# Attention values in four column groups of the PE array, with the first 64-key product carrying values and sums together

## The chip, the cores and the metric

One core of a Trainium2 chip runs the kernel. The time is device microseconds of one execution, the median of several runs. Engines are named as the profile names them: PE (matmul; PEld is its weight load), DVE (vector), ACT (scalar), POOL, SP, and the DMA queues that SP and POOL issue to.

## The reference, cut to what matters

Attention over 4 batches, 12 heads, 448 positions and 64 channels, all float32, with a soft cap on the scores, followed by a two-layer network with squared ReLU:

```
scores = cap * tanh(scale * q @ k.T / cap)
p      = exp(scores - max)
attn   = p / (sum(p) + 1e-9)
y      = attn @ v                       # (4, 12, 448, 64)
x      = heads of y side by side        # (1792, 768)
out    = (max(x @ w_in, 0) ** 2) @ w_out  # 768 -> 2048 -> 768
```

## The kernel before, in words

The program has three stages. The attention stage treats 24 pairs of heads (two heads of one batch fill the 128 partitions, 64 channels each). The second and third stages are the two matrix products of the network, in a Strassen form; a planner writes out their order from costs and due times, and starts with leftovers of attention (the last normalisations). The first units of the second stage run on PE straight behind the last pair.

The attention loop (L597) is software-pipelined by hand, and each engine executes its instructions in the order written. In cycle n:

- PE computes the scores of pair n transposed (keys on partitions), in three pieces of 128 keys (`scores`, L397) and, in even cycles, the remaining 64 keys of this pair and the next one in one piece (`half_scores`, L404). Then it multiplies the probabilities of pair n-1 with the values: `pv_half` (L437) opens the two accumulators `pa` (values of both heads) and `pb` (sums of the probabilities, by a matrix of ones) with the 64-key piece; `sums` (L448) adds to `pb`, by four 32-column matmuls, what DVE has added up of the other three pieces; `pv` (L455) adds those pieces to `pa`, with two 64-column matmuls for each.
- ACT applies tanh to each score piece and exp to two tiles a cycle; in cycles 5 to 16 it casts a finished x as well (L509), and now and then it decodes a piece of `w_in`.
- DVE adds the probability tiles (`add_p`, `add_p3`), transposes the next queries and keys (`turn_kq`, L390), copies `pb` out (`take_sums`, L467) and `pa` out (`evac`, L462), inverts the sums (`invert`, L474) and multiplies (`normalise`, L493).
- The sums travel: two DMAs on SP take them from one row for each half of the queries to a compact tile of 32 x 28 (`cmp`), which DVE inverts, a third puts it to DRAM (`rd`), and two on POOL (`spread`, L482) copy it to 64 partitions each, beside the values in `e`, where `normalise` finds it one cycle later.

`pa` and `pb` are one PSUM bank each and single-buffered; the `es` tile that `take_sums` writes is single-buffered too. `e` has three buffers. The kernel alternates the halves of partitions that the two heads' last 64 keys occupy from pair to pair (`rows`, `v_slot`, L364 to L376).

Of the kernel before, what the change touches and what calls it, by code (L numbers as in the profile page):

```python
# [240 lines left out]
def tile_softcap_attention_mlp(ctx, tc, q, k, v, cap, w_in, w_out, out):  # L241
# [42 lines left out]
    ep = rctx.enter_context(tc.tile_pool(name="ep", bufs=2))  # L284
    scr = rctx.enter_context(tc.tile_pool(name="scr", bufs=1))
# [13 lines left out]
    guard = const.tile([P, 1], F32, name="guard")  # L299
# [10 lines left out]
    vn = [keep.tile([P, NS + 1, D], F32, name=f"vn{i}") for i in range(NKV)]  # L310
# [4 lines left out]
    def prepare():  # L315

        nc.vector.memset(ones, 1.0)

# [4 lines left out]

    def fetch_w(pool, f, first, bufs):
        raw = new_raw(pool, bufs)
        if first:
            nc.sync.dma_start(
                out=raw.rearrange("p (c f) -> p c f", f=P),
                in_=w_in[:, f * P:(f + 1) * P].rearrange("(c p) f -> p c f", p=P),
            )  # L330
        else:
            nc.sync.dma_start(out=raw, in_=w_out[f * P:(f + 1) * P])
        return raw
# [18 lines left out]
    top, bottom = slice(0, D), slice(D, P)  # L352

    def load_part(n, i, a, queue):
        b, j = divmod(n, NPAIR)
        h, w = divmod(a, 2)
        x = (k, q)[i][b, 2 * j + h, :, 32 * w:32 * w + 32].rearrange("(t r) e -> r t e", r=32)
        queue.dma_start(out=kqn[n % NKQ][32 * a:32 * a + 32, i], in_=x)  # L358
# [5 lines left out]
    def rows(n, h):  # L364
        return bottom if (n + h) % 2 else top

    def keys(n, h, u):
        odd = (n + h) % 2
        if u:
            return slice(odd * D + (u - 1) * P, odd * D + u * P)  # L370
        return slice(0, D) if odd else slice(3 * P, S)

    def v_slot(n, h, u):
        if n % 2 == 0:
            return (0, 4)[h] + u - 1 if u else 3
        return (1, 4)[h] + u - 1 if u else (0, 7)[h]  # L376

    def load_v(n):
        b, j = divmod(n, NPAIR)
        x = v[b, 2 * j:2 * j + 2].rearrange("h (t r) d -> (h t) r d", r=D)  # L380
        for i in range(2):
            r, at = (bottom, 0) if (n + i) % 2 else (top, n % 2)
            nc.gpsimd.dma_start(out=vn[n % NKV][r, at:at + NS], in_=x[i::2].rearrange("t r d -> r t d"))  # L383
# [13 lines left out]
    def scores(n, u):  # L397
        sc = ps_s.tile([P, 2, 512], F32, tag="s", name="sc")
        kt, qt = kqs[n][:, :S], kqs[n][:, S:]
        for h, r in enumerate((top, bottom)):  # L400
            nc.tensor.matmul(out=sc[:, h, :S], lhsT=kt[r, keys(n, h, u)], rhs=qt[r], start=True, stop=True)  # L401
        probs[n, u] = sc

    def half_scores(n):  # L404
        sc = ps_s.tile([P, 2, 512], F32, tag="s", name="sc")
        for i in range(2):
            kt, qt = kqs[n + i][:, :S], kqs[n + i][:, S:]
            for h, r in enumerate((top, bottom)):
                nc.tensor.matmul(out=sc[rows(n + i, h), i, :S], lhsT=kt[r, keys(n + i, h, 0)], rhs=qt[r],  # L409
                                 start=True, stop=True)  # L410
# [26 lines left out]
    def pv_half(n):  # L437
        pvs[n, 0] = ps_v.tile([P, S], F32, tag="pa", name="pa")
        pvs[n, 1] = ps_v.tile([P, S], F32, tag="pb", name="pb")
        p = probs.pop((n, 0))  # L440
        for h, o in enumerate((top, bottom)):
            r = rows(n, h)
            nc.tensor.matmul(out=pvs[n, 0][o], lhsT=vn[n % NKV][r, v_slot(n, h, 0)], rhs=p[r], start=True, stop=False)  # L443
        for h, o in enumerate((bottom, top)):
            r = rows(n, h)
            nc.tensor.matmul(out=pvs[n, 1][o], lhsT=ones[r], rhs=p[r], start=True, stop=False)

    def sums(n):  # L448
        a = adds.pop(n)
        for i in range(4):  # L450
            h, c = 1 - i // 2, slice(i % 2 * HS, (i % 2 + 1) * HS)
            nc.tensor.matmul(out=pvs[n, 1][32 * i:32 * i + 32, c], lhsT=ones[:, :32], rhs=a[:, h, c],  # L452
                             start=False, stop=True, tile_position=(0, 32 * i))

    def pv(n):  # L455
        for u in range(1, NU):
            p = probs.pop((n, u))
            for h, r in enumerate((top, bottom)):
# [850 lines left out]
```

## Time and profile before

| | us |
|---|---|
| median of 3 runs (586.91 to 587.23) | 586.96 |
| the profiled execution, its time | 587.03 |
| the profiled execution, its span | 585.4 |
| PE busy in the span | 576.9 |
| DVE busy | 463.8 |
| ACT busy | 380.2 |
| POOL busy | 156.1 |

Busy time of PE is modelled and says little by itself; the attention stage lies between about 8 and 175 us of the span, and what follows is the network. How busy an engine is has to be read by stage: the rows below give it in pieces of the attention loop.

### The profile page before, as it was taken

The numbers are of one execution on the slowest core, as the hardware profiler recorded it, in microseconds if no ns is written. First come the engines' busy times: TensorE is split into PE (matmuls) and PEld (weight loads), VectorE is DVE, ScalarE is ACT, GpSimd is POOL, SyncE is SP. The second block draws the span as 40 slices with busy tenths as digits, with TensorE's granted clock in tenths as the row PEclk, the third lists the DMA queues.
The fourth block names the chain that finished last, engine by engine and source line by source line (L and its number), as shares of the span: only waits on it lengthen the run. The fifth ranks groups of instructions, "written<-read, shape, count | busy, mean of one in ns | idle before, by whom it ended". The sixth has DMA issues, their size and how long they took to land.

```text
span 585.4 us, 9055 instructions
## 1 busy us (share of the span) xinstructions
PE 576.9 (99%) x3286; PEld 458.2 (78%) x3286; DVE 463.8 (79%) x607; ACT 380.2 (65%) x437; POOL 156.1 (27%) x245
## 2 busy tenths in 40 slices
PE   8999999999999999999999999999999999999996
PEld 5333333333349999999999999999999999999996
DVE  2778889899969989979789983756899996766651
ACT  4999999999958877577667763765635543333230
POOL 8688787886421001120211211100000000000000
PEclk9999999999999999999999999999999999999999
DMA  9989999899215235886879778997899236544511
GB/s 133 134 160 167 172 179 156 171 156 171 83 51 161 111 117 203 261 269 225 265 243 330 241 264 302 318 335 255 247 279 289 71 109 209 148 142 146 169 40 45
DMA packets 138997, 110.18 MB, mean 188 GB/s; under 512 B 53728, under 2 KB 127968, under 8 KB 138944
## 3 DMA queue, kind: packets, MB, share of 16 engines
q1 hardware_dynamic: 125408, 71.86, 46.9%
q0 software_dynamic: 12000, 37.39, 23.3%
q8 instruction: 27, 0.44, 0.3%
q10 hardware_dynamic: 1536, 0.27, 0.3%
q14 instruction: 26, 0.21, 0.1%
HBM read 82.84 MB, written 26.56 MB: 187 GB/s over the span
## 4 chain that ended last, share of the span: by engine, by line
PE 93%; DMA 2%; DVE 2%; ACT 1%; issue 0%; SPq 0%; POOL 0%; ACTq 0%; DVEq 0%; POOLq 0%
PE hps L349 35%; PE po L1141 35%; PE pa L459 9%; PE sc L401 8%; PE pa L443 3%; PE pb L452 2%; PE sc L409 1%; DMA cap_sb<-in_cap_dram 1%; DMA cmp<-es 1%; ACT p L427 1%; ACT p L419 1%; DMA wraw<-in_moe_w_in_dram 1%; DVE es L469 0%; SPq L472 0%; POOL kqn L358 0%
## 5 line engine op out<-in xcount | busy, mean ns | idle before, releaser
L1141 PE MATMUL po<-th,gh 128*128 128x384 f32 x728 | 190.2, 336 | 0.0
L1141 PEld LDWEIGHTS po<-th,gh 128*128 128x128 f32 x728 | 131.9, 188 | 0.0
L1141 PE MATMUL po<-th,gl 128*128 128x384 f32 x392 | 131.7, 336 | 0.0
L1130 ACT CAST gh<-a 128x1024 fp32r<-128x1024 f32 x47 | 49.4, 1052 | 97.3 <-PE po L1141 90.4
L349 PE MATMUL hps<-xt,op 128*128 128x448 f32 x450 | 92.4, 362 | 0.0
L349 PEld LDWEIGHTS hps<-xt,op 128*128 128x128 f32 x450 | 84.4, 187 | 5.6
L419 ACT ACTIVATE p<-sc 128x896 f32<-128x896 f32 x84 | 73.4, 908 | 10.2 <-PE sc L401 10.0
L1141 PEld LDWEIGHTS po<-th,gl 128*128 128x128 f32 x392 | 73.7, 188 | 0.0
L427 ACT ACTIVATE p<-p 128x1792 f32<-128x1792 f32 (+1 forms) x48 | 72.5, 1511 | 1.3
L1131 DVE TENSOR_TENSOR gl<-a,gh 128x1024 fp32r<-128x1024 f32 x47 | 57.4, 1222 | 19.0 <-ACT gh L1130 19.0
L349 PE MATMUL hps<-xs,op 128*128 128x448 f32 x324 | 67.6, 363 | 0.0
L349 PEld LDWEIGHTS hps<-xs,op 128*128 128x128 f32 x324 | 60.6, 188 | 5.4 <-issue 1.4
L401 PE MATMUL sc<-kq 64*128 64x448 f32 x288 | 61.0, 555 | 0.9 <-DVE kq L394 0.7
L358 POOL DMA_DIRECT2D kqn<-in_k_dram x92 | 59.0, 648 | 2.5 <-issue 1.5
L459 PE MATMUL pa<-p,vn 128*64 128x448 f32 x288 | 59.4, 548 | 0.0
L401 PEld LDWEIGHTS sc<-kq 64*128 64x128 f32 x288 | 25.6, 186 | 35.4 <-issue 18.6
L349 PE MATMUL hps<-xh,op 128*128 128x448 f32 x168 | 49.4, 362 | 0.0
L383 POOL DMA_DIRECT2D vn<-in_v_dram x48 | 35.2, 739 | 31.8 <-PE pa L459 31.4
L459 PEld LDWEIGHTS pa<-p,vn 128*64 128x64 f32 x288 | 18.5, 136 | 30.9 <-issue 30.9
L1154 DVE TENSOR_TENSOR osb<-s,po 128x384 f32<-128x384 f32 x27 | 14.9, 552 | 27.4 <-PE po L1141 27.3
L48 DVE CUSTOM_DVE_ANT_0 wf<-wraw,wf 128x1536 uint16<-128x1536 uint16 x32 | 30.4, 949 | 3.7 <-ACT wraw L43 1.7
L40 ACT ACTIVATE wf<-wraw 128x768 f32<-128x768 f32 x32 | 29.1, 911 | 6.3 <-DVE op L831 4.3
(94 smaller groups left out, 838.5 us busy)
## 6 DMA issues: line engine op xcount, KB each, us to landing
a<-g_dram SPq DMA_DIRECT2D x56, 512.0 KB
wraw<-in_moe_w_out_dram SPq DMA_DIRECT2D x16, 768.0 KB
wraw<-in_moe_w_in_dram SPq DMA_DIRECT2D x12, 768.0 KB
g_dram<-r POOLq DMA_DIRECT2D x18, 448.0 KB, 5.0
g_dram<-u POOLq DMA_DIRECT2D x14, 448.0 KB, 5.1
w_dram<-wf POOLq DMA_DIRECT2D x16, 384.0 KB, 5.9
vn<-in_v_dram POOLq DMA_DIRECT2D x48, 112.0 KB, 4.3
e<-rd POOLq DMA_DIRECT2D x48, 112.0 KB, 3.7
```

Of the source, the lines that this page charges most:

```text
L40: size=lambda: nc.scalar.activation(out=magf, in_=high.bitcast(F32), func=ACTF.Abs, scale=2.0 ** 16),
L48: total=lambda: V.tensor_tensor(out=mag, in0=mag, in1=low, op=ALU.add),
L349: nc.tensor.matmul(out=out, lhsT=w, rhs=x[:, j], start=start and c == 0 and s == 0, stop=stop and c == NHALF - 1 and s == 2, skip_group_ch ...
L358: queue.dma_start(out=kqn[n % NKQ][32 * a:32 * a + 32, i], in_=x)
L383: nc.gpsimd.dma_start(out=vn[n % NKV][r, at:at + NS], in_=x[i::2].rearrange("t r d -> r t d"))
L401: nc.tensor.matmul(out=sc[:, h, :S], lhsT=kt[r, keys(n, h, u)], rhs=qt[r], start=True, stop=True)
L419: nc.scalar.activation(out=p, in_=probs[n, u][:, :, :S], func=ACTF.Tanh, scale=by["qks"])
L427: nc.scalar.activation(out=p, in_=p, func=ACTF.Exp, scale=by["cap"])
L459: nc.tensor.matmul(out=pvs[n, 0][r], lhsT=vn[n % NKV][:, v_slot(n, h, u)], rhs=p[:, h], start=False, stop=(u == NU - 1))
L1130: last["act"] = nc.scalar.copy(out=hi, in_=x)
L1131: last["dve"] = nc.vector.tensor_sub(out=lo, in0=x, in1=f32(hi))
L1141: last["mm"] = nc.tensor.matmul(out=po, lhsT=w[:, c], rhs=m[:, cols], start=(c == 0 and i == 0), stop=(c == HF - 1 and i == 2))
```

## The change

The probabilities' sums and values now share one accumulator of two banks, `pv`, one bank for each head. Head 1's values lie on partitions 0 to 63 of bank 1 and head 0's on partitions 64 to 127 of bank 0; the other half of each bank takes the sums. The value tile gets a column block of ones at both ends, so that `pv_half` is two matmuls of 64 rows by 128 columns (values and sums together) in place of four of 64 by 64. `pv` uses four matmuls of 32 columns for each piece of 128 keys in place of two of 64, and runs ahead of `sums`. One DVE instruction over both banks, `evac`, adds the guard (1e-9, on the rows of sums only) and copies; `take_sums` and its tile are gone. Two DMAs collect two full rows of 448 each, so that `cmp` has 64 rows; it is inverted at the end of the next cycle, and `spread` is issued at the end of a cycle, in POOL's order still behind the same loads. Heads no longer alternate by pair where the values are concerned, but in the places of queries and keys (`head`); the rows of `w_in` are fetched with their halves of 64 exchanged, by two transfers for each column block. The planner's ready times for the last two pairs change with it.

```diff
+    def head(n, place):
+        return place if n % 2 else 1 - place
...
     def pv_half(n):
-        pvs[n, 0] = ps_v.tile([P, S], F32, tag="pa", name="pa")
-        pvs[n, 1] = ps_v.tile([P, S], F32, tag="pb", name="pb")
+        pvs[n] = ps_v.tile([P, 2, 512], F32, tag="pv", name="pv")
         p = probs.pop((n, 0))
-        for h, o in enumerate((top, bottom)):
-            r = rows(n, h)
-            nc.tensor.matmul(out=pvs[n, 0][o], lhsT=vn[n % NKV][r, v_slot(n, h, 0)], rhs=p[r], start=True, stop=False)
-        for h, o in enumerate((bottom, top)):
-            r = rows(n, h)
-            nc.tensor.matmul(out=pvs[n, 1][o], lhsT=ones[r], rhs=p[r], start=True, stop=False)
+        for h, slot in enumerate((0, NS + 1)):
+            w = vn[n % NKV][rows[h], slot:slot + 2].rearrange("p t d -> p (t d)")
+            nc.tensor.matmul(out=pvs[n][:, h, :S], lhsT=w, rhs=p[rows[h]], start=True, stop=False)
...
     def pv(n):
         for u in range(1, NU):
             p = probs.pop((n, u))
-            for h, r in enumerate((top, bottom)):
-                nc.tensor.matmul(out=pvs[n, 0][r], lhsT=vn[n % NKV][:, v_slot(n, h, u)], rhs=p[:, h],
-                                 start=False, stop=(u == NU - 1))
+            for i in range(4):
+                h, c = 1 - i // 2, quarter(i % 2)
+                nc.tensor.matmul(out=pvs[n][quarter(i), h, :S], lhsT=vn[n % NKV][:, 1 + 3 * h + u, c], rhs=p[:, h],
+                                 start=False, stop=(u == NU - 1), tile_position=(0, 32 * i))
...
     def evac(n):
-        es[n] = ep.tile([P, 2, S], F32, tag="u", name="e", bufs=3)
-        nc.vector.tensor_copy(out=es[n][:, 0], in_=pvs.pop((n, 0)))
-
-    def take_sums(n):
-        e = ep.tile([P, S], F32, tag="es", name="es", bufs=1)
-        nc.vector.tensor_scalar(out=e, in0=pvs.pop((n, 1)), scalar1=guard, scalar2=None, op0=ALU.add)
+        e = es[n] = ep.tile([P, 2, S], F32, tag="u", name="e", bufs=3)
+        nc.vector.tensor_tensor(out=e, in0=pvs.pop(n)[:, :, :S], in1=guard.unsqueeze(2).to_broadcast([P, 2, S]), op=ALU.add)
         rds[n] = ep.tile([NC, HB], F32, tag="cmp", name="cmp", bufs=NE)
-        for c in range(2):
-            nc.sync.dma_start(out=rds[n][c * (NC // 2):(c + 1) * (NC // 2)], in_=e[32 * c:P:64, c * HS:(c + 1) * HS])
+        for h in range(2):
+            nc.sync.dma_start(out=rds[n][h * NC // 2:(h + 1) * NC // 2], in_=e[D * h:D * h + D:32, h])
...
     for n in range(NP + 1):
...
-        if n >= 3:
-            spread(n - 3)
...
-        if n >= 2:
-            invert(n - 2)
...
         if old:
+            pv(n - 1)
             sums(n - 1)
-            take_sums(n - 1)
+        if old:
             fetch_early(n)
-            pv(n - 1)
...
         split_low(n - 5)
+        if n >= 3:
+            spread(n - 3)
         if old:
             evac(n - 1)
+        if n >= 2:
+            invert(n - 2)
...
-    spread_a = do("POOL", 0.7, lambda: spread(NP - 2), ready=4.0, lag=6.5)
-    invert_b = do("DVE", 0.6, lambda: invert(NP - 1), ready=6.5, lag=2.5)
+    spread_a = do("POOL", 0.7, lambda: spread(NP - 2), ready=8.5, lag=6.5)
+    invert_b = do("DVE", 0.6, lambda: invert(NP - 1), ready=9.2, lag=3.0)
```

## Rows read from the trace of the kernel before

**Rows 1.** The page: chain of work that ended last, shares by engine.

```profile
PE 93%; DMA 2%; DVE 2%; ACT 1%; issue 0%; SPq 0%; POOL 0%; ACTq 0%; DVEq 0%; POOLq 0%
```

**Rows 2.** That chain in order of time, two cycles: start us, us, what.

```profile
100.55 2.46 PE sc L401 x12
...
103.00 0.52 PE pa L443 x2
...
103.91 0.75 PE sc L409 x8
104.67 0.52 PE pb L452 x8
105.18 2.41 PE pa L459 x12
107.59 2.46 PE sc L401 x12
...
113.88 2.46 PE sc L401 x12
```

**Rows 3.** Timeline, PE weight loads: start us, us; in brackets idle time before.

```profile
110.88 0.16 PEld L452 LDWEIGHTS pb<-add,ones 128*32 128x32 f32 x8 [0.70 <-DVE add L434]
...
111.83 0.14 PEld L459 LDWEIGHTS pa<-p,vn 128*64 128x64 f32 x2 [0.23 <-issue]
```

**Rows 4.** Busy time by window of whole pairs of cycles, attention.

```profile
20.08:33.42 13.34, 13.34 (x91) 4.74 (x90) 10.42 (x14) 12.87 (x12) 9.80 (x15) 1.00 0.84 132
33.42:73.40 39.98, 39.98 (x266) 14.18 (x266) 32.72 (x46) 37.11 (x38) 33.12 (x51) 1.00 1.02 167
73.40:100.55 27.15, 26.77 (x180) 9.48 (x178) 24.95 (x38) 26.91 (x29) 21.46 (x32) 1.00 1.05 172
100.55:113.88 13.33, 13.33 (x90) 4.73 (x90) 11.92 (x19) 12.51 (x14) 10.42 (x16) 1.00 0.81 158
113.88:127.24 13.36, 13.36 (x90) 4.73 (x90) 12.87 (x20) 13.23 (x15) 10.61 (x16) 1.00 1.00 162
127.24:153.90 26.66, 26.66 (x178) 9.46 (x178) 24.94 (x39) 25.77 (x25) 16.11 (x24) 1.00 0.79 149
153.90:167.23 13.33, 13.33 (x90) 4.73 (x89) 11.92 (x19) 12.34 (x12) 5.58 (x10) 1.00 0.20 64
```

**Rows 5.** Groups by line and form, ACT, 20 to 175 us: mean ns, idle before.

```profile
L419 ACT ACTIVATE p<-sc 128x896 f32<-128x896 f32 x78 | 68.2, 908 | 5.2 <-PE sc L401 5.0
L427 ACT ACTIVATE p<-p 128x1792 f32<-128x1792 f32 x33 | 56.0, 1698 | 1.1
L427 ACT ACTIVATE p<-p 128x896 f32<-128x896 f32 x12 | 11.4, 951 | 0.2
```

**Rows 6.** Groups by line and form, DVE, 20 to 175 us.

```profile
L434 DVE TENSOR_TENSOR add<-add,p 128x896 f32<-128x896 f32 x23 | 25.0, 1085 | 4.1 <-ACT p L427 3.8
...
L469 DVE TENSOR_SCALAR es<-pb,guard 128x448 f32<-128x448 f32 x23 | 15.5, 676 | 11.1 <-PE pb L452 11.1
L464 DVE COPY e<-pa 128x448 f32<-128x448 f32 x24 | 14.8, 618 | 3.5 <-PE pa L459 2.9
```

**Rows 7.** Timeline, the copy of `pa` and the next product.

```profile
115.62 0.62 DVE L464 COPY e<-pa 128x448 f32<-128x448 f32 x1
...
116.29 0.14 PEld L443 LDWEIGHTS pa<-p,vn 64*64 64x64 f32 x2 [0.68 <-DVE e L464]
```

**Rows 8.** The chain again, the slowest gathering of sums.

```profile
72.35 4.62 DMA cmp<-es
```

**Rows 9.** Waits of POOL, 20 to 175 us: us, times, longest.

```profile
POOL vn L383 <- PE pa L459: 31.4, 21, 4.1
```

**Rows 10.** Timeline behind attention: last inversion, spreading, normalisation, PE's next product.

```profile
178.54 0.31 DVE L476 RECIPROCAL cmp<-cmp 32x28 f32<-32x28 f32 x1
...
181.96 1.22 POOL L485 DMA_DIRECT2D e<-rd  x2
...
185.72 6.56 PE L349 MATMUL hps<-xt,op 128*128 128x448 f32 x32
...
186.71 0.61 DVE L499 TENSOR_TENSOR xf<-e 128x448 f32<-128x448 f32 x1
...
190.24 1.09 DVE L770 TENSOR_TENSOR xt<-xf,xt 128x896 fp32r<-128x896 f32 x1
```

More of the change, by code (lines that the diff above doesn't have):

```diff
@@ L298, in tile_softcap_attention_mlp @@
     far = const.tile([1, 1], I32, name="far")
-    guard = const.tile([P, 1], F32, name="guard")
+    guard = const.tile([P, 2], F32, name="guard")
     keep = actx.enter_context(tc.tile_pool(name="keep", bufs=1))
@@ L309, in tile_softcap_attention_mlp @@
     kqn = [keep.tile([P, 2, NT32, 32], F32, name=f"kqn{i}") for i in range(NKQ)]
-    vn = [keep.tile([P, NS + 1, D], F32, name=f"vn{i}") for i in range(NKV)]
+    vn = [keep.tile([P, NS + 3, D], F32, name=f"vn{i}") for i in range(NKV)]
     ones = keep.tile([P, D], F32, name="ones")
@@ L317, in prepare @@
         nc.vector.memset(ones, 1.0)
+        for t in vn:
+            nc.vector.memset(t[:, ::NS + 2], 1.0)
     xs, xt = {}, {}
@@ L322, in new_raw, with w_rows @@
         return pool.tile([P, DM], U64, tag="wraw", name="wraw", bufs=bufs)
+    top, bottom = slice(0, D), slice(D, P)
+    rows = bottom, top
+    def w_rows(f):
+        return w_in[:, f * P:(f + 1) * P].rearrange("(c h p) f -> h p c f", h=2, p=D)
     def fetch_w(pool, f, first, bufs):
@@ L326, in fetch_w @@
         if first:
[L327 to L330, printed above, removed]
+            for h, r in enumerate(rows):
+                nc.sync.dma_start(out=raw[r].rearrange("p (c f) -> p c f", f=P), in_=w_rows(f)[h])
         else:
@@ L399, in scores @@
         kt, qt = kqs[n][:, :S], kqs[n][:, S:]
-        for h, r in enumerate((top, bottom)):
-            nc.tensor.matmul(out=sc[:, h, :S], lhsT=kt[r, keys(n, h, u)], rhs=qt[r], start=True, stop=True)
+        for i, r in enumerate((top, bottom)):
+            h = head(n, i)
+            nc.tensor.matmul(out=sc[:, h, :S], lhsT=kt[r, keys(h, u)], rhs=qt[r], start=True, stop=True)
         probs[n, u] = sc
@@ L407, in half_scores @@
             kt, qt = kqs[n + i][:, :S], kqs[n + i][:, S:]
-            for h, r in enumerate((top, bottom)):
-                nc.tensor.matmul(out=sc[rows(n + i, h), i, :S], lhsT=kt[r, keys(n + i, h, 0)], rhs=qt[r],
-                                 start=True, stop=True)
+            for a, r in enumerate((top, bottom)):
+                h = head(n + i, a)
+                nc.tensor.matmul(out=sc[rows[h], i, :S], lhsT=kt[r, keys(h, 0)], rhs=qt[r], start=True, stop=True)
         probs[n, 0] = sc
@@ L483, in spread @@
         rd = rds.pop(n)
[L484 to L486 removed]
+        for h, r in enumerate(rows):
+            halves = rd[h].rearrange("r c q -> (r c) q")[::3]
+            nc.gpsimd.dma_start(out=es[n][r, 1 - h].rearrange("p (c q) -> p c q", c=2),
+                                in_=halves.partition_broadcast(D))
     def x_of(half, i, c):
@@ L573, in fetch_early @@
                     raws[f] = new_raw(scr, 2)
-                for c in (2 * (n - at), 2 * (n - at) + 1):
-                    nc.sync.dma_start(out=raws[f][:, c * P:(c + 1) * P], in_=w_in[c * P:(c + 1) * P, f * P:(f + 1) * P])
+                c = 2 * (n - at)
+                for h, r in enumerate(rows):
+                    nc.sync.dma_start(out=raws[f][r, c * P:(c + 2) * P].rearrange("p (c f) -> p c f", f=P),
+                                      in_=w_rows(f)[h, :, c:c + 2])
     raws = {}
@@ L580, in tile_softcap_attention_mlp @@
     HB = 28
-    NC = 2 * S // HB
+    NC = 4 * S // HB
     START, DEEP = 9, 3
```

56 lines of the change are left out of this document (25 added, 31 removed).

## The prediction

> **What bounds the kernel now.** I began with the chain that ended last, by engine [rows 1]: 93% of the span is PE. So I read PE in the attention loop, where the change lies, from the chain in order of time [rows 2]. The reader is to see that PE's pieces follow each other without a gap. The even cycle runs from 100.55 to 107.59, which is 7.04 us, and the odd one from 107.59 to 113.88, which is 6.29 us; together 13.33. Then I asked how far off the other engines are, in windows of whole pairs of cycles [rows 4]. ACT is busy 12.51 of 13.33 us in one, 13.23 of 13.36 in another, and 26.91 of 27.15 between 73.40 and 100.55, where PE itself is short of full for once (26.77). So PE sets the pace, and ACT stands right behind it, in three of the eleven pairs with nothing to spare. Behind attention PE is the chain as well, so what attention saves should reach the end whole.
>
> **What a cycle of PE consists of.** `half_scores` (L409) comes behind products of its own shape, 64x64, and takes 0.75 us for two rounds (each float32 matmul is two instructions): 0.375 a round of 448 columns, with four matmuls at once [rows 2]. By that, six rounds of scores are 2.25 of their 2.46 us, six of `pv` 2.25 of 2.41, two of `pv_half` 0.75 of 0.91 (103.00 to 103.91), and two half-length rounds of `sums` 0.375 of 0.52. What is left over, 0.21, 0.16, 0.16 and 0.15, stands at each change of tile shape: 64x128 to 64x64 to 128x32 to 128x64 and back, four of them in every cycle.
>
> **The change on PE.** The work in rounds stays the same. `pv_half` as two 64x128 matmuls is two rounds if both run at once, as the scores do; `pv` is six rounds if its four column groups run at once. What changes is the number of shape changes.
>
> - Odd cycles: scores and `pv_half` now have one shape (0.16 saved), `pv` and `sums` too (0.15 saved): 0.31.
> - Even cycles: the same two are saved, but `half_scores` is now of another shape than `pv_half` ahead of it (0.16 more): 0.15.
>
> That makes 0.46 for two cycles; since the first product of a shape still needs its weights in place, I take 0.43. Over eleven pairs [rows 4] it is 4.7 us, and the last cycle, where network products stand in the middle, saves the step from `sums` to `pv`, 0.15. If PE alone counted, with the 0.38 us that it lacks in the third window, this would be 5.3 us.
>
> The trace does not show 128x32 matmuls over 448 columns. The bounds: all four at once, 0.375 us a round, as `sums` (four column groups, 224 columns) keeps to 0.52 and `half_scores` runs four 448-column matmuls at once; or two at a time, 0.75 a round, 2.25 us more in a cycle. I take the lower end, nearest to both rows. The weight loads double in number: eight loads of 32 columns take 0.16 us together, 0.08 a round of four, and two of 64 columns take 0.14 and lie inside a round, followed by 0.23 of idle [rows 3]. So I cost them at nothing, hidden by the round in progress.
>
> Here a rule speaks against the change. The Trainium skill, "TensorE: Matmul & The Clock Gate", Part 3, says that a weight load overlaps a running matmul only when the two differ in row group. Column groups of 128 rows share all of theirs, so by it `pv`'s loads would stand in the open. The pairs of 64 columns in [rows 3] speak against the rule: their loads sit within rounds that still follow each other at 0.375. By the rule the change would lose time; that is the third rival.
>
> **What ACT lets through.** ACT's work is unchanged. Its idle time is 0.47, 2.87, 0.24, 0.82, 0.13, 0.89 and 0.99 us in the seven windows [rows 4], which hold 1, 3, 2, 1, 1, 2 and 1 pairs of cycles. Not all of it can be used: exp's own idle, 1.1 and 0.2 us [rows 5], is the step from one ACT instruction to the next that needs it, and 1.3 over 11 pairs is 0.12 a pair. The other 5.2 is tanh waiting, 5.0 of it for PE's scores, just what a faster PE removes. So a window saves the smaller of PE's 0.43 a pair and ACT's idle time less 0.12 a pair: 0.35, 1.29, 0, 0.43, 0.01, 0.65 and 0.43, in sum 3.2. The last cycle has no ACT work in its way: 0.15. **Sum: 3.3 us.** The saving of PE in the first cycle (`pv` no longer waits there for the added probabilities) I leave out, since ACT sets the start.
>
> **The change on DVE.** The two copies, 676 + 618 ns, become one instruction over 896 columns [rows 6]. No row has it with PSUM and a broadcast operand; the bounds are one half-width copy, 0.62, and both of before, 1.29. I take 1.09, the tensor_tensor of 896 columns, which is nearest in form. DVE gets 0.2 us a cycle back. It is not on the path on average: its fullest window is 12.87 of 13.36 [rows 4].
>
> Its place matters more. One accumulator of two banks means that `pv_half` of the next pair waits until this copy is done, and behind the copy on DVE stand the inversion and then `add_p3` of the next cycle, for which only `sums` waits, now 2.4 us later in PE's order than before. Between the last product and the next `pv_half` PE has 2.46 us of scores [rows 2]. A copy of 1.09 with some 0.1 us of hand-over may therefore start 1.27 late without cost. Before, the copy of `pa` started at 115.62, 1.74 after PE's product ended at 113.88 [rows 2, 7], among the latest in the trace, and PE went on right behind it at 116.29. But `take_sums` (0.68) and the inversion (0.31 in [rows 10]) no longer stand ahead of it: 1.74 less 0.99 is 0.75, within the 1.27. Cost nothing; without that relief the stall would be 0.5 in such a cycle.
>
> **The way of the sums.** They now leave half a cycle later and are inverted a full cycle later. The gathering took 4.62 us at its slowest [rows 8], and a cycle has 6.4, so the inversion does not wait. The queue on SP orders the gathering behind the copy, then the inverted sums, then the next cycle's loads of queries, which are wanted more than a cycle later. `spread` keeps its place in POOL's order, behind the key loads, but its data come later; POOL waited 31.4 us in 21 cycles for PE before its value loads [rows 9], 1.5 a cycle, and a delay up to that costs nothing. `normalise` comes more than half a cycle after. The bytes gathered double, but they are the smallest transfers of the loop. I cost all of this at nothing, hidden by that slack; without it, each us by which the normalised x of a pair came late would delay DVE's copy behind it, and PE once the 1.27 is gone.
>
> Behind attention, where the last pair's way cannot be hidden by another cycle, the inversion ran at 178.54, `spread` at 181.96, `normalise` at 186.71 [rows 10]. The products on that x are the third unit of the run that begins at 185.72; at 18 instructions of 0.2 us each (6.56 for 32) that is about 193.0, and the split operand is ready at 191.33. So there are 1.7 us of room. DVE reached the inversion late by its own order, so the new way (copy at about 176, inversion about 180) is 1.5 later at most. Cost 0, upper end 1 us.
>
> The added ones, the three small guard instructions and the rows of `w_in` in two transfers lie at the start, where DVE waits for loads, and on SP's queue long ahead of use: nothing.
>
> **The rivals.**
>
> - ACT gives way: its idle time counts in full, and gaps shrink where the engines hand over faster. Then PE's own 5.3 us arrives: 581.7. For it, DVE is lighter, and PE's loss in the third window began with a late DVE copy; against it, ACT's 26.91 of 27.15 there.
> - The gain is eaten: copies late by more than 1.27 us, or ACT out of step. To cancel 3.3 us in 23 cycles takes 0.14 a cycle. About 586.9. For it, the copy now waits for the last product and is longer; against it, the relief of 0.99 ahead of it.
> - Column groups' weight loads in the open: 0.08 us a round [rows 3], six rounds, 0.48 a cycle, less the 0.215 saved: 0.27 a cycle, about 6 us in 23 cycles, slower: 593. It decides from 0.036 us a round on (0.215 / 6). This is what the sum comes to by that rule of the skill; the two-group rounds of `pv` speak against it, and they have only half as many loads.
>
> **How the numbers follow.** The sum stands against the profiled execution: 587.03 - 3.3 = 583.7, and the median of the runs lies 0.07 lower, so 583.7 stays. Chances: forecast 0.66 (own range 582.2 to 585.4), ACT gives way 0.12, eaten 0.12, loads in the open 0.10. A measurement of this kernel can tell about 0.2% from no change, 1.2 us. Faster by more: 0.66 + 0.12 = 0.78; within 0.2%: 0.12; slower: 0.10. The range takes in the first three, from 581.5 to 587.2, and leaves the last out; the upper end of 1 us behind attention lies in it.
>
> **What the profile after would show.** Chain in order of time: odd cycles near 6.0 us and even ones near 6.9 where ACT has room; scores straight into `pv_half` at 0.75; `pv` at 2.4 and `sums` at 0.38 behind it. Idle time of tanh before PE's scores falls from 5.0 to under 2. The copy takes 1.09 us and no product waits for it. Wrong it would be if `pv` took 2.9 or more (loads in the open), if the next `pv_half` waited for the copy in most cycles, or if PE stood still between 190 and 195 us for the last x.

## The result and the profile after

The change made the kernel slower: median 595.41 us (593.2 to 595.92) against 587.1 in the same session (586.91 to 588.57), ratio 1.0129 [1.0098, 1.016]. The profiled execution took 593.2 us, its span is 591.6 (before 587.03 and 585.4). It is the fastest of the four (the others took 594.91 to 595.92, and no trace shows where they lost more), and the account below is that of this run.

First the page's chain of work that ended last, shares by engine. Against the 93% of [rows 1], PE is down to 70%, and transfers, DVE and SP's queue have come in: PE no longer sets the pace alone.

```profile
PE 70%; DMA 14%; DVE 7%; SPq 3%; POOL 2%; issue 2%; ACT 2%; DVEq 0%; POOLq 0%; ACTq 0%
```

The chain in order of time, late in the loop (start us, us, what), answers [rows 2]:

```profile
154.73 1.10 DVE e L468
...
155.88 1.02 PE pv L446 x4
156.90 0.91 PE sc L413 x8
157.81 2.39 PE pv L456 x24
160.21 0.38 PE pv L463 x8
160.58 2.46 PE sc L404 x12
163.04 0.75 PE pv L446 x4
163.79 2.39 PE pv L456 x24
166.19 0.38 PE pv L463 x8
```

An odd cycle is now 2.46 + 0.75 + 2.39 + 0.38 = 5.98 us, an even one with its 0.91 is 6.89: 12.87 for two where [rows 2] give 13.33. PE's saving is there. The first line shows the other side: the copy ended at 155.83, later than PE wanted it, and a `pv_half` that had to wait takes 1.02 instead of 0.75. So each stop costs 0.27 beyond the wait itself.

Groups by line and form, 20 to 175 us (busy, mean ns, idle before and its releaser), which answer [rows 5] and [rows 6]:

```profile
L446 PE MATMUL pv<-p,vn 64*128 64x448 f32 x92 | 22.0, 556 | 3.4 <-DVE e L468 2.7 <-ACT p L422 0.7
...
L422 ACT ACTIVATE p<-sc 128x896 f32<-128x896 f32 x77 | 67.2, 907 | 3.7 <-PE sc L404 3.3
...
L468 DVE TENSOR_TENSOR e<-pv,guard 128x896 f32<-128x896 f32 x24 | 26.1, 1086 | 8.4 <-PE pv L463 7.8
...
L385 POOL DMA_DIRECT2D vn<-in_v_dram x42 | 30.9, 740 | 4.7 <-PE pv L456 3.2 <-DMA kqn<-in_k_dram 0.6 <-issue 0.5
```

And one line of the waits there (us, times, longest), against [rows 9]:

```profile
POOL e L485 <- DMA rd<-cmp: 30.0, 13, 4.9
```

PE stops in front of `pv_half`, mostly for the copy. POOL's slack before the value loads, 31.4 us in [rows 9], is down to 3.2; POOL now stands 30.0 us in front of `spread` for the stored sums, with the next pairs' loads behind it.

Busy time by window (PE, PEld, DVE, ACT, POOL with instructions; granted clock; DMA share; GB/s), which answers [rows 4]. Over 20 to 160 us PE stands 3.4 us, where [rows 4] show 0.38:

```profile
60.00:80.00 20.00, 18.80 (x150) 6.76 (x150) 15.74 (x21) 18.41 (x20) 14.29 (x22) 1.00 1.10 170
80.00:100.00 20.00, 19.39 (x156) 7.23 (x152) 19.13 (x26) 19.82 (x22) 16.06 (x26) 1.00 1.09 170
...
20.00:160.00 140.00, 136.59 (x1088) 51.41 (x1088) 121.22 (x161) 134.29 (x135) 102.67 (x156) 1.00 0.94 156
```

What is left of PE's saving shows in the timeline of PE, from the first scores after 19 us to the network products that stand in the last cycle: 22 cycles, before and after.

```profile
20.01 2.53 PE L401 MATMUL sc<-kq 64*128 64x448 f32 x12
...
167.16 3.88 PE L349 MATMUL hps<-xs,op 128*128 128x448 f32 x18
```

```profile
19.54 2.53 PE L404 MATMUL sc<-kq 64*128 64x448 f32 x12
...
166.49 3.88 PE L357 MATMUL hps<-xs,op 128*128 128x448 f32 x18
```

That is 147.15 us before and 146.95 after: eleven pairs at 0.46 should save 5.1 us, and 0.2 is left. By the starts of their scores, eight of the 22 cycles are longer than 5.98 or 6.89, by 5.4 us together: 3.4 of standing in five of them, and 0.27 in each of the seven whose `pv_half` had to wait. (Before, such waits cost 0.5.) Besides, the change reaches the first of these scores 0.5 us sooner. So the network's long run of products begins at 174.03 instead of 174.80. From there to the end of the span it is 417.6 us, before 410.6. **The 7 us are lost behind attention.** The timeline there (POOL's and DVE's instructions, SP's issues; in brackets idle before), against [rows 10]:

```profile
181.01 0.31 DVE L475 RECIPROCAL cmp<-cmp 64x28 f32<-64x28 f32 x1
...
181.35 0.50 SPq L477 DMA_DIRECT2D rd<-cmp  x1
182.08 5.95 SPq L338 DMA_DIRECT2D wraw<-in_moe_w_in_dram  x4
...
187.05 1.21 POOL L485 DMA_DIRECT2D e<-rd  x2 [6.32 <-DVE wf L41]
...
194.53 0.63 DVE L499 TENSOR_TENSOR xf<-e 128x448 f32<-128x448 f32 x1 [5.28 <-DMA e<-rd]
...
196.21 1.49 PE L357 MATMUL hps<-xt,op 128*128 128x448 f32 x3 [3.11 <-DVE xt L776]
...
198.34 4.48 PE L357 MATMUL hps<-xt,op 128*128 128x448 f32 x11 [0.64 <-DVE xt L776]
```

The last inversion runs 2.5 us later than in [rows 10], but `spread` goes out 5.1 later and the last x is normalised 7.8 later. From 182.08 to 188.03, around `spread`, four fetches of `w_in` go out on SP. The windows around it:

```profile
184.00:194.00 10.00, 9.10 (x46) 8.19 (x44) 5.18 (x7) 5.54 (x7) 1.78 (x3) 1.00 1.08 236
194.00:196.00 2.00, 0.00 (x0) 0.00 (x0) 1.47 (x2) 0.81 (x1) 0.00 (x0) 0.98 0.13 52
196.00:198.00 2.00, 1.49 (x3) 0.83 (x3) 1.97 (x3) 1.64 (x3) 0.00 (x0) 0.50 0.00 0
198.00:200.00 2.00, 1.67 (x5) 1.49 (x6) 1.97 (x3) 1.93 (x3) 0.00 (x0) 0.50 0.00 0
200.00:202.00 2.00, 2.00 (x7) 1.78 (x6) 1.93 (x4) 1.56 (x2) 0.00 (x0) 0.50 0.00 0
202.00:204.00 2.00, 2.00 (x10) 1.83 (x9) 1.97 (x4) 1.34 (x3) 0.00 (x0) 0.82 0.00 0
```

The DMA engines are full (1.08) and PE stands for 0.90 + 2.00 + 0.51 + 0.33 = 3.7 us, 3.11 of it in one stop. Behind that stop it works at a granted clock of 0.50, the lower of its two levels (1.2 GHz), which makes half of 1.49 + 1.67 + 2.00 worthless, 2.6 us, and 0.4 more in the last window. Together 6.7 of the 7.0.

### The profile page after: what moved, and what is told of

Same layout as the page of the kernel before. It is cut to its first block, busy times and chain, and to the rows that moved or that the text cites. A ratio compares the mean times of both kernels' runs of the same rounds, so it can differ in the third digit from the quotient of the medians.

```text
span 591.6 us, 9480 instructions
## 1 busy us (share of the span) xinstructions
PE 576.3 (97%) x3478; PEld 461.8 (78%) x3478; DVE 460.1 (78%) x589; ACT 379.7 (64%) x437; POOL 155.9 (26%) x245
## 4 chain that ended last, share of the span: by engine, by line
PE 70%; DMA 14%; DVE 7%; SPq 3%; POOL 2%; issue 2%; ACT 2%; DVEq 0%; POOLq 0%; ACTq 0%
PE po L1147 34%; PE hps L357 32%; DMA kqn<-in_k_dram 4%; DMA kqn<-in_q_dram 3%; DMA rd<-cmp 3%; DMA wraw<-in_moe_w_in_dram 2%; PE pv L456 2%; DVE add L437 2%; SPq L368 1%; DMA e<-rd 1%; DVE xt L776 1%; POOL kqn L368 1%; ACT p L430 1%; POOL e L485 1%; DVE cmp L475 1%
## 5 line engine op out<-in xcount | busy, mean ns | idle before, releaser
L357 PE MATMUL hps<-xt,op 128*128 128x448 f32 x450 | 95.6, 369 | 3.7 <-DVE xt L776 3.7
L357 PEld LDWEIGHTS hps<-xt,op 128*128 128x128 f32 x450 | 86.1, 192 | 10.6 <-DVE xt L776 4.7
L456 PE MATMUL pv<-p,vn 128*32 128x448 f32 x576 | 59.1, 543 | 0.0
L456 PEld LDWEIGHTS pv<-p,vn 128*32 128x32 f32 x576 | 16.3, 109 | 39.8 <-issue 39.8
L485 POOL DMA_DIRECT2D e<-rd x48 | 29.4, 616 | 53.2 <-DMA rd<-cmp 35.7
```

The lines of the kernel that those rows point to most:

```text
L357: nc.tensor.matmul(out=out, lhsT=w, rhs=x[:, j], start=start and c == 0 and s == 0, stop=stop and c == NHALF - 1 and s == 2, skip_group_ch ...
L456: nc.tensor.matmul(out=pvs[n][quarter(i), h, :S], lhsT=vn[n % NKV][:, 1 + 3 * h + u, c], rhs=p[:, h], start=False, stop=(u == NU - 1), til ...
L485: nc.gpsimd.dma_start(out=es[n][r, 1 - h].rearrange("p (c q) -> p c q", c=2), in_=halves.partition_broadcast(D))
```

## The experiments

All change the kernel after unless said otherwise. "Attention ends" is the start of the network's long run of products in the profiled execution; the last two columns are PE's busy us there.

| run | median us | ratio to before | attention ends | 20 to 160 | 180 to 200 |
|---|---|---|---|---|---|
| before (profiled 587.03) | | | 174.80 | 139.62 | 20.00 |
| the change | 595.41 | 1.0129 [1.0098, 1.016] | 174.03 | 136.59 | 16.25 |
| e1_hold | 593.03 | 1.0103 [1.0086, 1.0119] | 175.76 | 134.51 | 17.14 |
| e2_old_ready | 590.05 | 1.0054 [1.0034, 1.0074] | 175.16 | 135.03 | 17.82 |
| e3_early_invert | 590.89 | 1.007 [1.0046, 1.0094] | 177.46 | 133.84 | 18.60 |
| e4_hold_early | 594.58 | 1.0133 [1.0116, 1.015] | 177.75 | 134.89 | 17.70 |
| e5_one_transfer | 590.35 | 1.006 [1.0043, 1.0077] | 176.12 | 135.33 | 18.16 |
| e6_before_groups | 585.1 | 0.997 [0.996, 0.998] | 174.22 | 136.71 | 20.00 |
| e7_one_fetch | 588.84 | 1.0031 [1.0016, 1.0045] | 177.26 | 133.49 | 18.43 |
| e8_still_sums | 588.41 | 1.0031 [1.0019, 1.0042] | 176.21 | 134.91 | 20.00 |
| e9_hold_for_landing | 586.88 | 0.9999 [0.9984, 1.0014] | 173.82 | 136.63 | 20.00 |
| e10_still_fetch4 | 586.68 | 0.9995 [0.9983, 1.0008] | 173.99 | 136.47 | 20.00 |
| e11_groups_fetch4 | 584.4 | 0.9959 [0.9944, 0.9974] | 172.27 | 138.64 | 20.00 |
| e12_hold_fetch4 | 586.33 | 0.9992 [0.9979, 1.0005] | 174.16 | 136.18 | 20.00 |
| e13_no_way | 587.34 | 1.0007 [0.9998, 1.0017] | 174.60 | 135.64 | 20.00 |
| e14_copy_sooner | 587.38 | 1.0004 [0.9989, 1.0018] | 174.88 | 137.02 | 20.00 |
| e15_few_values | 584.01 | 0.9959 [0.9945, 0.9973] | 172.14 | 137.83 | 20.00 |
| e16_groups_copy_sooner | 585.98 | 0.9984 [0.9975, 0.9994] | 174.20 | 136.93 | 20.00 |
| e17_before_few_values | 587.4 | 1.0013 [1.0003, 1.0022] | 174.50 | 139.62 | 20.00 |
| e18_thin_values | 583.97 | 0.9947 [0.993, 0.9964] | 171.79 | 138.13 | 20.00 |

One profile says little of the loop: in e1, e2, e7 and e9 the attention loop is that of the change, and yet attention ends between 173.82 and 177.26. Where such ends differ by less than 3 us, the medians have to decide. The way from there to the end of the span is steady: 410.3 to 411.6 us in every run in which PE is full from 180 to 200, 417.6 in the change.

### Behind attention: order, wait, or transfers

**e1_hold**: the planner lets the fetches go no sooner than its clock's 20.

```diff
-            h.fetch, here = transfer("SP", fetch, 768, due=at - 16.0, ready=at - early, take="raw")
+            h.fetch, here = transfer("SP", fetch, 768, due=at - 16.0, ready=max(at - early, 20.0), take="raw")
```

> The changed kernel, with the planner's w_in fetches behind attention held until 20 us on its clock, so that none is in flight while the last pair's inverted sums are written and spread. Theory A (the last normalisation came at 194.5 instead of 186.7 us because its two small transfers shared the 16 DMA engines with the w_in fetches; PE stood about 3.7 us and then ran some 6 us at half clock): the last normalisation comes before 189, PE has no wait between 185 and 200, the clock stays full, and the time falls by about 7 us to 586 to 588. Theory B (the planner's later order of the inversion alone makes it late): the last spread still lands after 191, and the time stays within 2 us of the changed kernel's 595. The loop of attention is untouched and should end at 174.1 as before the edit.

Only the order changed: the fetches went out right behind the inverted sums, at 183.63, `spread` at 186.17 landed after 8.31 us, and the last x was normalised at 195.18. Fetches ordered later on a queue still run beside it. By its numbers theory B holds, but the wait that theory A asks for was never made, so the run does not decide between them.

**e2_old_ready** gives the planner the due times of before:

```diff
-    spread_a = do("POOL", 0.7, lambda: spread(NP - 2), ready=8.5, lag=6.5)
-    invert_b = do("DVE", 0.6, lambda: invert(NP - 1), ready=9.2, lag=3.0)
+    spread_a = do("POOL", 0.7, lambda: spread(NP - 2), ready=4.0, lag=6.5)
+    invert_b = do("DVE", 0.6, lambda: invert(NP - 1), ready=6.5, lag=2.5)
...
-    spread_c = do(None, 0.0, lambda: None, ready=8.0)
+    spread_c = None
```

> The changed kernel with the planner's ready times and lags of the kernel before (spread 4.0, inversion 6.5, no time for the third normalisation). Theory A (shared DMA engines): the inversion comes some 2 us sooner, but the fetches still lie beside the transfers; the gain is under 3 us, 592 to 596. Theory B (the planner's order): the last normalisation is back near 187 and the time near 587. A third theory, that DVE, which executes in order, now waits on the inversion and delays the second stage: slower than 596.

The inversion moved to 179.55, but `spread` still went out at 186.18 and the last x was normalised at 192.33. PE stood 2.2 us and kept its clock. At 590.05 the run lies between the two forecasts: the planner's order is worth 5.4 us of the median, but the last x is still 5.6 later than before (186.71).

**e3_early_invert** moves `invert(n - 2)` from behind `evac` to behind `add_p`, ahead of `normalise`; **e4_hold_early** is that and e1.

> The changed kernel with the inversion of pair n-2 ahead of the normalisation in DVE's cycle n, in place of behind the copy. Theory L (in the loop the inverted sums leave so late that POOL's spreading waits for them, the normalisation waits 6.2 us in sum for the spreading, the copy behind it comes late, and PE waits 3.4 us for the copy): DVE's wait for the spreading and PE's for the copy fall under 1 us each, and attention ends 2 to 3 us sooner, 171 to 172; the time falls by as much, to about 593, if the tail stays as it is. Rival M (ACT's lack of idle time is what limits the loop, and the waits only move): attention ends within 0.7 us of 174.1.

> Both edits: fetches of w_in held, inversion ahead of the normalisation. If theories A and L hold and do not overlap: 7 + 2.5 us off the changed kernel's 595, about 584 to 585.5, which is faster than the kernel before (587). If the loop's gain is eaten by ACT: about 587.

In e3's loop (20 to 175 us) DVE's wait for the spread sums, 6.2 us in the change, is gone, but DVE now waited 10.9 us for the gathering, 8.8 of it in nine waits on the transfer itself. The wait had only moved one step up the sums' way. Attention ended at 177.46 and 177.75, so theory L and its rival both missed.

**e5_one_transfer** and **e7_one_fetch** fetch `w_in` over 128 partitions at a time again; rows of `w_in` are then not exchanged to suit the new places of the heads, so the output is not the reference's. e5 does it everywhere, e7 behind attention alone:

```diff
-            for h, r in enumerate(rows):
-                nc.sync.dma_start(out=raw[r].rearrange("p (c f) -> p c f", f=P), in_=w_rows(f)[h])
+            nc.sync.dma_start(
+                out=raw.rearrange("p (c f) -> p c f", f=P),
+                in_=w_in[:, f * P:(f + 1) * P].rearrange("(c p) f -> p c f", p=P),
+            )
```

> The changed kernel with w_in fetched in transfers over all 128 partitions again, as before the change (the rows' halves are not exchanged, so head 0's values meet head 1's rows of w_in). Theory P (a transfer to 64 partitions moves at 200 to 280 GB/s where one to 128 partitions moved at 350 to 420 between 176 and 194 us, so the exchange by halves keeps the DMA engines busy about twice as long just when the last sums are spread, and in cycles 6 to 20): the last normalisation comes before 190, PE has no wait behind attention, the granted clock stays full; time 586 to 588, and lower if the loop's waits for the sums fall too. Rival Q (the sums' way is too long by itself): the last normalisation still after 191, time above 591.

> As the run with whole transfers, but only for the fetches behind attention; the early fetches in cycles 6 to 20 stay in halves. Theory P: the tail is mended all the same (time within 2 us of that run), and the difference between the two in where attention ends is what the halves cost in the loop: 0 to 2 us.

Both are faster than the change by 5 to 6.6 us. In their profiles the last x was normalised at 194.10 and 194.97, hardly otherwise than in the change, but attention had ended 2.1 and 3.2 us later; from its end to that of the span it is 413.1 and 414.6 us instead of 417.6. So halves cost something, 4.5 and 2.9 us of it behind attention, as far as one profile of each tells (that of e7 took 593.48, and its runs spread from 585.65 to 593.48). What a half costs shows where hardly anything else runs: transfers of halves in e9 (below), and under it whole ones in the kernel before, beside the end of a store (windows; the last two columns are DMA share and GB/s).

```profile
196.00:198.00 2.00, 2.00 (x11) 1.87 (x11) 1.93 (x4) 1.90 (x3) 0.00 (x0) 1.00 1.15 204
```

```profile
192.00:193.00 1.00, 1.00 (x7) 0.94 (x6) 0.96 (x2) 1.00 (x3) 0.00 (x0) 1.00 1.06 377
```

By these two windows the same bytes in halves keep the engines full for nearly twice as long.

**e8_still_sums**: every `spread` reads the first pair's inverted sums (the output is not the reference's), so none waits for its own pair.

```diff
-        rd = dram.tile([2, 2, 2, HS], F32, tag="rd", name="rd")
+        rd = dram.tile([2, 2, 2, HS], F32, tag="rd" if n else "rk", name="rd", bufs=2 if n else 1)
...
-        rds[n] = rd
+        rds.setdefault("kept", rd)
...
     def spread(n):
-        rd = rds.pop(n)
+        rd = rds["kept"]
```

> The changed kernel where the spreading of every pair reads the inverted sums of pair 0, so that it waits for no inversion of its own (the normalisation of the other pairs is by pair 0's sums; inversion and its transfers still run). Theory L (the sums' way delays the normalisation, the copy and PE): DVE's wait for the spreading goes, PE's wait for the copy falls from 3.4 to under 1 us, attention ends 2 us or more before 174.1, and the tail is mended as well, since the last spreading can go at once: 584 to 588. Rival: PE's waits for the copy stay near 3 us (DVE is late by its own work), attention ends at 173.5 to 174.5; then only the tail gains.

The end is mended (PE full from 180 to 200), so it is the last pair's way that PE stood for. In the loop the theory fell: PE's waits for the copy are 5.1 us. The longest, 3.5, has another cause: at 74.94 ACT had waited 3.36 us for an early piece of `w_in`, and copy and PE with it.

**e9_hold_for_landing**: small transfers on SP's queue read the last spread sums; the fetches stand behind them and so cannot start before the landing.

```diff
+    mark = dram.tile([2, 1], F32, name="mark", bufs=1)
+
+    def landed():
+        e = es[NP - 1]
+        for h in range(2):
+            nc.sync.dma_start(out=mark[h:h + 1], in_=e[D * h:D * h + 1, h, 0:1])
+
+    landed_b = do("SP", 0.7, landed, spread_b, lag=0.0)
...
-            h.fetch, here = transfer("SP", fetch, 768, due=at - 16.0, ready=at - early, take="raw")
+            h.fetch, here = transfer("SP", fetch, 768, landed_b, due=at - 16.0, ready=at - early, take="raw")
```

> The change with one addition: small transfers on SP's queue that read the last pair's spread sums, so that the transfers of w_in behind attention start only when the last spreading has landed. Theory (the end costs what it does because the last gathering, fetch and spreading share the DMA engines with w_in): the last normalise begins by 189 instead of 194.5, TensorE has no stall of several us behind attention and no stretch at half clock, 587 to 589 us. Rival (the sums' way is as long without w_in beside it): the normalise still begins after 193, and the time is 592 or more.

Its timeline, to hold against the change's above:

```profile
180.81 0.31 DVE L475 RECIPROCAL cmp<-cmp 64x28 f32<-64x28 f32 x1
...
184.14 1.21 POOL L485 DMA_DIRECT2D e<-rd  x2 [3.62 <-DVE xf L800]
...
188.15 4.61 SPq L338 DMA_DIRECT2D wraw<-in_moe_w_in_dram  x6
189.50 0.62 DVE L499 TENSOR_TENSOR xf<-e 128x448 f32<-128x448 f32 x1
```

The inversion comes at the same time as in the change, the last x 5.0 us sooner; PE neither stands nor loses its clock, and 8.5 us of median are back. The DMA share from 184 to 194 us is 0.58 instead of 1.08. The theory holds: the time, 586.88, lies just below its range and the normalise begins half a microsecond later than it says. The loop is as in the change: attention ends at 173.82.

### The loop: sums, copies, loads

**e6_before_groups** makes one part of the change alone, on the kernel before; **e11_groups_fetch4** adds the sooner early fetch of `w_in`:

```diff
-            for h, r in enumerate((top, bottom)):
-                nc.tensor.matmul(out=pvs[n, 0][r], lhsT=vn[n % NKV][:, v_slot(n, h, u)], rhs=p[:, h],
-                                 start=False, stop=(u == NU - 1))
+            for i in range(4):
+                h, c = i // 2, i % 2 * 32
+                nc.tensor.matmul(out=pvs[n, 0][32 * i:32 * i + 32], lhsT=vn[n % NKV][:, v_slot(n, h, u), c:c + 32],
+                                 rhs=p[:, h], start=False, stop=(u == NU - 1), tile_position=(0, 32 * i))
...
-    FETCH = 6, 9, 14, 18
+    FETCH = 4, 9, 14, 18
```

> The kernel before with one part of the change alone: pv in four column groups of 32, nothing else moved. It saves one change of tile shape a cycle, between sums and pv: 0.15 us in 24 cycles. Theory: 1.5 to 3.6 us faster than before (583.2 to 585.3), ACT's idle time taking the rest; a cycle's pv stays at 2.3 to 2.4 us. Rival: no change within 0.2%, if ACT takes it all.

> The kernel before with the values in four column groups alone, and the early transfers of w_in two cycles sooner. Theory: ScalarE's 1.1 us of waiting for an early piece of w_in goes, 584 to 585 us. Rival (that wait is hidden): as without the sooner transfers, 585.1.

Both came as forecast and beat the kernel before and the change, e11 by 2.6 us (0.41%) against before. ACT's wait for `w_in`, 1.1 us in e6, is gone in e11. This is the best version with the reference's output that was run.

**e10_still_fetch4** and **e12_hold_fetch4** put the same `FETCH` into e8 and e9.

> The kernel whose pairs all take the first pair's inverted sums (its output is not the reference's), with the early transfers of w_in issued two cycles sooner. Theory (what the loop loses is the wait for the sums' way and for an early piece of w_in): with both gone attention ends near 172 and the time is 584 to 585 us. Rival (the loop is held by ScalarE or by the values' copies, whatever lands when): attention ends at 174.5 or later and the time stays above 586.

> The change with w_in behind attention held until the last spreading has landed, and the early transfers of w_in two cycles sooner. Theory (the two losses add): 585.5 to 588 us, below the kernel with the hold alone by 1 to 2. Rival (the early transfers only move which cycle is late): within 0.5 of the kernel with the hold alone.

ACT's wait for `w_in` goes in both. e10 gains 1.7 us on e8, but at 586.68 it is above the 584 to 585 of its theory, which fell; e12 is 0.55 below e9, which is nearly what its rival allows (0.5) and not the 1 to 2 of its theory. PE stands for the copy 3.5 and 3.8 us.

**e13_no_way**, also with the new `FETCH`, leaves out gathering and store of the inverted sums after the first pair (the output is not the reference's):

```diff
+        if n:
+            return
         for h in range(2):
             nc.sync.dma_start(out=rds[n][h * NC // 2:(h + 1) * NC // 2], in_=e[D * h:D * h + D:32, h])
...
     def invert(n):
-        cmp = rds[n]
+        cmp = rds[0]
         nc.vector.reciprocal(out=cmp, in_=cmp)
+        if n:
+            return
```

> The change with the gathering and the store of the inverted sums done for the first pair alone; every later cycle still inverts and spreads that pair's sums (its output is not the reference's), and the early transfers of w_in go two cycles sooner. No instruction of VectorE waits for a gathering any more. Theory (the loop lost its gain to the sums' way): TensorE's waits for the copy fall under 1.5 us, attention ends at 170 to 171.5 and the time is 582 to 584 us. Rival (the loop is held by the loads of the next pairs or by ScalarE, which the shorter cycles run into): attention ends at 173 or later, the time is 585 to 587, and the waits in front of the late copies name the keys' or queries' loads or ScalarE.

My theory until then fell: POOL has its slack back (16.1 and 7.9 us in front of the value loads), and the time is 587.34, with attention's end at 174.60. But `spread` still runs in every cycle, and DVE still waits 4.0 us for its landing. A stretch of the chain names what else is late, the keys' loads:

```profile
37.04 5.56 DMA kqn<-in_k_dram
...
44.58 1.12 DVE kq L396
...
45.85 0.62 POOL kqn L368
46.47 6.98 DMA kqn<-in_k_dram
```

**e14_copy_sooner** (on e12) and **e16_groups_copy_sooner** (on e11) put `normalise`, `split_low`, `spread` and `evac` ahead of `add_p` in DVE's order.

> The change with w_in held until the last spreading has landed and its early transfers two cycles sooner, and on VectorE the normalisation and the copy of values and sums put ahead of the next pair's addition, which waits for ScalarE. Theory (copies come late because VectorE does that addition first, when ScalarE is late): TensorE's waits for the copy fall from 3.8 to under 1.5 us, attention ends at 171 to 172.5, 583 to 585 us. Rival (VectorE is then idle while it waits for the values and is late with the addition and the next transposition instead): 586 or more.

> The kernel before with the values in four column groups, w_in two cycles sooner, and the same order on VectorE: normalisation and copy ahead of the addition. Theory of the late addition: the remaining 1.7 us of waits for copy and ScalarE shrink, 583.2 to 584.2. Rival: 584.4 or more.

Neither helped, as the rivals said: in e14 DVE's copy then waits 12.3 us for PE (15 to 205 us; 8.0 in e12) and its normalisation 7.9 for the spread sums (3.8 in e12), and in e16 `sums` stands 2.4 us for the late addition. The order as it was is the better one.

**e15_few_values** (on e12) and **e17_before_few_values** (on before) load no values after the first three (`n < 2`) and six pairs (`n < 5`); **e18_thin_values** (on e12) keeps every transfer but moves one block of seven (in all three the output is not the reference's).

```diff
-        if prep:
+        if prep and n < 2:
             load_v(n + 1)
```

```diff
-            nc.gpsimd.dma_start(out=vn[n % NKV][r, 1 + i:1 + i + NS], in_=x[i::2].rearrange("t r d -> r t d"))
+            t = NS if n < 3 else 1
+            nc.gpsimd.dma_start(out=vn[n % NKV][r, 1 + i:1 + i + t], in_=x[i::2][:t].rearrange("t r d -> r t d"))
```

> The same kernel with the order as in the change, but with values loaded for the first three pairs alone (later pairs use theirs again; the output is not the reference's): 42 transfers of 112 KB and 31 us of GpSimd's time fall away. Theory (the shorter cycles run into the loads: GpSimd waits for the sums with the next pair's loads behind it, and the DMA engines are full): attention ends at 171 to 172.5, 583 to 584.5 us, and the keys land sooner. Rival (the copy and ScalarE hold the loop, not the loads): attention ends at 173 or later and the time stays within 0.7 of 586.3.

> The kernel before with values loaded for the first six pairs alone (its output is not the reference's): the control for the run without the values' loads. TensorE of the kernel before stands 0.4 us in the loop, so by the theory of the loads it gains under 0.7: 586.3 to 587. If it gains 1.5 or more, the loads hold the kernel before as well.

> The change with w_in held and sooner, and from the fourth pair on only one of seven blocks of values in each transfer (its output is not the reference's): GpSimd issues the same instructions and waits in the same places, the bytes of the values are down by six sevenths. Without the values' transfers the time was 584.0 and attention ended at 172.2; with them whole it was 586.3 and 174.2. Theory (the DMA engines are full): as without them, attention ends at 171.5 to 172.7, 583.7 to 584.8. Rival (GpSimd's own time and its order hold the keys' loads back): attention ends at 173.5 or later, 585.5 or more.

Windows of e12 and, below it, of e18:

```profile
20.00:160.00 140.00, 136.18 (x1086) 51.35 (x1087) 120.63 (x161) 133.90 (x135) 103.05 (x156) 1.00 0.93 156
```

```profile
20.00:160.00 140.00, 138.13 (x1106) 52.74 (x1104) 122.98 (x164) 135.78 (x136) 95.00 (x158) 1.00 0.61 128
```

With the DMA share down from 0.93 to 0.61, PE works 1.95 us more in this stretch, and the median falls by 2.4 us, from 586.33 to 583.97. POOL's own time falls too, by 8 us (103.05 to 95.00); but in e15 it falls by 31 (to 72.08) and the time is the same, 584.01, so it is the bytes and not POOL's time. The kernel before gains nothing from the same cut (587.4, a little above its forecast): its PE was not waiting for loads. But e18 is not free of waits: PE still stands 1.8 us for the copy, at 22.44, 88.12 and 115.04.

## Why the prediction was wrong

**Right: PE's cycles.** 0.43 us for two cycles was predicted, 0.46 came. `pv` takes 2.39 us, so the rival of weight loads in the open is out; that its price, 593, is the profiled time is chance. The timeline of the weight loads, against [rows 3]: a round's four loads take 0.13 us and PEld has idled 0.25 ahead of them.

```profile
164.12 0.13 PEld L456 LDWEIGHTS pv<-p,vn 128*32 128x32 f32 x4 [0.25 <-issue]
```

The rule of the Trainium skill, "TensorE: Matmul & The Clock Gate", Part 3, that asks for different row groups does not hold for these loads; the trace decides.

**Right: the copy's price. Not settled: ACT's share.** The copy takes 1086 ns (1.09 taken). Tanh's idle time before PE's scores fell from 5.0 to 3.3 us, not under 2. With the end mended and the DMA engines relieved (e18) the time is 583.97, close to the forecast of 583.7, but that is partly luck: attention ends 3.0 us sooner there than before, and 0.6 of it comes from the first cycle, which the prediction had left out.

**Wrong, first step: "Then I asked how far off the other engines are."** I read ACT in [rows 4] and passed over the last but one column of the same rows: a DMA share of 1.02, 1.05 and 1.00 in three windows. The shorter cycles want the same loads sooner from engines that are full; without the bytes, the loop gets 2.4 us back (e18 against e12). What lands late differs from stop to stop. In one of the change's five stops it is the keys, whose transposition stands right ahead of the copy:

```profile
20.64 1.11 DVE L396 STREAM_TRANSPOSE kq<-kqn 128x896 f32<-128x896 f32 x1 [0.42 <-DMA kqn<-in_k_dram]
...
21.68 1.05 DVE L468 TENSOR_TENSOR e<-pv,guard 128x896 f32<-128x896 f32 x1
...
22.79 1.02 PE L446 MATMUL pv<-p,vn 64*128 64x448 f32 x4 [0.72 <-DVE e L468]
```

In the next two it is the spread sums, for which the normalisation ahead of the copy waited:

```profile
66.97 0.63 DVE L499 TENSOR_TENSOR xf<-e 128x448 f32<-128x448 f32 x1 [2.17 <-DMA e<-rd]
...
69.23 1.02 PE L446 MATMUL pv<-p,vn 64*128 64x448 f32 x4 [0.68 <-ACT p L422]
...
73.80 0.62 DVE L499 TENSOR_TENSOR xf<-e 128x448 f32<-128x448 f32 x1 [1.50 <-DMA e<-rd]
...
76.01 1.02 PE L446 MATMUL pv<-p,vn 64*128 64x448 f32 x4 [0.53 <-DVE e L468]
```

(At 69.23 the profile names ACT, whose tanh ended at 69.08; the copy ended at 69.13.) DVE waits 6.2 us for spread sums in the loop; in e12 it is 3.8, and in e18 the wait is gone.

**Wrong in the same step: the copy's place, "Cost nothing".** The last of the five stops has no transfer ahead of it:

```profile
113.20 1.09 DVE L434 TENSOR_TENSOR add<-p 128x896 f32<-128x896 f32 x1 [0.79 <-ACT p L430]
...
115.81 1.08 DVE L468 TENSOR_TENSOR e<-pv,guard 128x896 f32<-128x896 f32 x1
...
116.95 1.02 PE L446 MATMUL pv<-p,vn 64*128 64x448 f32 x4 [0.82 <-DVE e L468]
```

The addition waited for ACT, and the copy behind it started 2.2 us after PE's last product, which ended at 113.60; the prediction allowed 1.27. The stop at 90.03 also follows DVE's own late work. Both stay in e18 (at 115.04 and 88.12). This is the rival "The gain is eaten", forecast at about 586.9: with the end mended, e9 takes 586.88.

The term was +3.3 for the loop. In the profile 0.2 came in its 22 cycles and 0.1 in the last, 3.0 short; the 0.5 of the first cycle brings it to 0.8. Open is why PE stands only 1.4 us in e11 (20 to 160 us), with its two copies and all the loads: whether by the room that a copy of half the length leaves, by the sums' smaller transfers, or by POOL's slack, no run tells apart.

**Wrong, second step: "Behind attention ... Cost 0, upper end 1 us."** It measured 7.0. The inversion was foreseen at about 180 and came at 181.01. What I left out is everything after it: that the stored sums and the spread ones share full DMA engines with `w_in` (e9), and that PE, after standing 3.11 us, works at a granted clock of 0.50. "if PE stood still between 190 and 195 us for the last x" was named as a sign, and it stood from 193.10 to 196.21. Waiting for the landing (e9) gives all of the 7.0 back; the due times of before (e2) or whole transfers (e5) alone give 4.3 and 4.5, mostly because PE's stops are shorter and its clock stays at 1.00.

**"The way of the sums ... at nothing"** was wrong as told: POOL's slack is used up, and DVE waits 6.2 us for spread sums in the loop and 5.28 behind it. How much of the loop's loss is due to it alone stays open: gathering and store cost no time that e13 could win back, but e13 still spreads. Altogether, for the profiled execution: 587.03 - 0.8 + 7.0 = 593.2.

**The two transfers of `w_in`: "nothing"** was wrong too: e5 and e7 win 5 to 6.6 us by undoing them, and halves move 204 GB/s on full engines where whole transfers move 377. So they are part of the 7.0: with more time on the engines, they meet the last sums for longer.

## What to carry to other kernels

When the bounding engine gets faster, read the DMA share of the same windows beside the next engine: here it was 1.0, and the bytes took 2.4 us of the shorter cycles' gain. Before a short chain of small transfers is put beside large ones, make the large ones wait for its landing, not merely follow it in a queue; that was worth 8.5 us here. Price a transfer in halves first; here a half moved at little more than half the rate. And try a change's parts alone: one part of this one, with a fetch moved two cycles, gave 584.4 us.

## What the hardware showed unexpectedly

- After PE had stood 3.11 us, up to 196.21, the granted clock was 0.50 from 196 to 202 us (with one more stop of 0.64) and 0.82 from 202 to 204, though PE worked; it was 1.00 again from 204. In e2 a stop of 2.18 left it at 1.00; in e1 it fell to 0.50 behind one of 2.03.
- The four 32-column loads of a round take 0.13 us and cost nothing in rounds of 0.375 us, although all their matmuls use the same 128 rows.
- A `pv_half` that PE had to wait for takes 1.02 us in the chain, one that follows other products 0.75.
- `w_in` in halves of 64 partitions moved at 204 GB/s with a DMA share of 1.15, whole at 377 with 1.06.
